# An mLSTM mixer on one core: loads in other shapes, a planner with later landings, priorities for each batch

## The chip, the cores and the metric

The kernel runs on one core of one Trainium2 chip. The time is device microseconds of the whole run. The core has five engines that each work off a list of instructions in order: TensorE (PE in the profile, with its weight loads as PEld), VectorE (DVE), ScalarE (ACT), GpSimd (POOL) and SyncE (SP), which here issues nearly all transfers. Transfers run on 16 DMA engines of the core. An instruction waits for semaphores of other engines or transfers, and all behind it on its engine wait with it.

## The reference

Four batches, eight heads, 768 tokens, 40 channels for each head. The first half is an mLSTM: a recurrence over tokens with a 40x40 state for each head and gates with a running maximum. The second half is a mixer over tokens of rank 32 and an MLP of 320 to 1280 to 320 channels with a residual.

```python
for t in range(S):
    m_new = np.maximum(f_gate[:, :, t] + m, i_gate[:, :, t])
    f_stab = np.exp(f_gate[:, :, t] + m - m_new); i_stab = np.exp(i_gate[:, :, t] - m_new); m = m_new
    C = f_stab[:, :, None, None] * C + i_stab[:, :, None, None] * np.einsum('bhd,bhe->bhde', vt, kt)
    n = f_stab[:, :, None] * n + i_stab[:, :, None] * kt
    nq = np.einsum('bhd,bhd->bh', n, qt)[:, :, None]
    y[:, :, t] = sigmoid(o_gate[:, :, t]) * np.einsum('bhde,bhe->bhd', C, qt) / np.maximum(np.abs(nq), 1.0)
x = y as (B, S, H * D)
u = x + ((x.transpose(0, 2, 1) @ U) @ V).transpose(0, 2, 1)
out = u + np.maximum(u @ w_ch1, 0.0) @ w_ch2
```

## The kernel before, in words

The tokens of a batch are cut into two halves of 384 and six chunks of 128. Heads go in groups of 3, 3 and 2, so a batch has six pieces (group and half), and 16 units (head and half). For a unit, VectorE builds the triangle of decays with a scan (L784, tile dm), TensorE the scores (q and k, L767), VectorE weighs the scores with the decays (L788, tile wt), and TensorE multiplies the result with v (tile tk). For a piece, k and weighted v give the state (tiles v and C), q is multiplied with its decays (L732, from tile fd) and with the state, the numerator is normed (L840) and gated into x (L845). When all six pieces of a batch are in x, the mixer over tokens follows (L872, tile pst; L917, tile ut), and then the MLP for each half of the batch: ten blocks of an up product (eight matmuls of ut with w1), a ReLU in a high part (ACT, L954) and a low part (DVE, L956), and three down products of three matmuls each (h with w2). Weights come as 64-bit words and are made into two 32-bit parts on ACT and DVE (L535 to L540, then L584, L585, L609).

Transfers: the token data of a piece (tk, L671, 544 or 363 KB), q of a piece (L676), q and k of a head and half (L756, 40 rows of 768 words, two of them side by side in tile qk), the decays of q of a piece (L729), the decays of a unit as one row copied to 128 partitions (L776), weights (L518). The gates are worked out first, for all batches, and stored: the decays of q in the DRAM tensor gsd (L463), those of the units in fsd (L444). The matrix V is stored once in DRAM (L559, tensor vsd) and read back in four copies (L569). The first 16 units take their decays from TensorE (L772) instead of a transfer.

The order of the instructions on all engines is made by a planner when the kernel is built (class Plan). Every operation has a kind, a priority, the engines it can run on, and a cost in ns. The planner steps through time, starts the ready operation of the lowest priority number on the engine that is free first, and writes each engine's list in the order of its own clock. An operation that both POOL and DVE can do goes to the one that would be done first. Where the planner expects TensorE to be idle or under-used, it puts in products of zeros (tile zeros, called fillers here). Tables add an offset to a kind's priority: ORDER for all batches, ORDER0 for the first.

Of the kernel before, what the change touches and what calls it, by code (L numbers as in the profile page):

```python
# [53 lines left out]
ORDER = {  # L54
    "gate": 20.0, "gate_w": 7.3, "part2": -70.0, "out_norm": -30.0, "part1": -10.0, "gate_turn": 10.0,
    "part3": -10.6, "rest1": 2.0, "w_low": 30.0, "vi": -10.0, "state": -4.0, "load_tk": -20.0, "load_qk": 0.9,
    "load_decay": -20.3, "w13_low": -30.0, "x_low": 24.0, "rows": -12.2, "inter": -1.6, "weigh": 1.8,
    "scores": 1.7, "weight_sign": -24.3, "weight_tail": 4.3, "cols": 21.8, "ut_high": 32.4, "store": 5.0,
    "decay_exp": -0.1,
}  # L60
ORDER0 = {
    "gate_w": 19.3, "part3": -44.0, "load_tk": 17.0, "load_q": -1.4, "x_low": -10.0, "rows": 25.0, "inter":
    -27.5, "weigh": 10.0, "scores": -4.1, "q_decay": 2.8, "weight_rebase": -20.9, "weight_sign": -23.3,
    "cols": 32.8, "store_g": 32.7, "residual": -7.0, "w_high": -27.4,
}
# [1035 lines left out]
```

## Time and profile before

| | us |
|---|---|
| runs of the kernel, median of 3 | 420.89 (420.51 to 435.31) |
| the profiled execution, whole | 416.58 |
| its span, first to last instruction | 414.8 |
| TensorE busy in the span | 393.2 |
| VectorE busy | 258.1 |
| GpSimd busy | 82.6 |
| mean granted TensorE clock | 0.97 of full speed |

A busy TensorE may be working at half its clock, or on fillers; both count as busy. A share of DMA is the mean over 16 engines: 0.20 is as much as three engines at work all the time and thirteen idle. The engines' queues run in order, so an engine's idle time has one cause at a time, the last thing that its next instruction waited for. Idle time of an engine off the longest chain costs nothing.

### The profile page before, as it was taken

What the parts mean: (1) busy time and instruction counts of PE and PEld (TensorE: products, weight loads), DVE (VectorE), ACT (ScalarE), POOL (GpSimd) and SP (SyncE); (2) the same over time, 40 slices, a digit from 0 to 9 for tenths busy, and PEclk for the clock granted to TensorE, in tenths of its full rate; (3) what the DMA queues carried; (4) which work ended last, traced back from release to release, by engine and by line L of the source; (5) the groups of instructions that cost most, each with busy time, mean ns of one, the idle gap of its engine ahead of it and who ended that gap; (6) DMA issues with size and microseconds to landing.
All of it is one profiled execution on the core that took longest, in us unless ns stands there. A gap on an engine that the chain in (4) does not pass through costs nothing.

```text
span 414.8 us, 7420 instructions
## 1 busy us (share of the span) xinstructions
PE 393.2 (95%) x2798; PEld 368.5 (89%) x2798; DVE 258.1 (62%) x534; ACT 124.6 (30%) x317; POOL 82.6 (20%) x96
## 2 busy tenths in 40 slices
PE   7995999998989999998899999999999999999995
PEld 5874888877888999987788999999999999999995
DVE  5996576999999965388798965328731233322132
ACT  4610323546345413212224232212421322111120
POOL 1652633125151600034323500003100000000000
PEclk9999558999999999999999999999999999999999
DMA  8746586867785361049665663102000010100001
GB/s 225 234 108 187 134 235 201 258 194 204 197 261 175 84 195 56 0 138 253 207 215 177 190 189 73 49 0 81 2 0 2 0 49 0 49 0 2 32 17 48
DMA packets 27260, 48.95 MB, mean 118 GB/s; under 512 B 3865, under 2 KB 18841, under 8 KB 27225
## 3 DMA queue, kind: packets, MB, share of 16 engines
q1 hardware_dynamic: 27032, 48.08, 40.4%
q8 instruction: 22, 0.36, 0.4%
q10 hardware_dynamic: 192, 0.40, 0.3%
q14 instruction: 14, 0.11, 0.1%
HBM read 44.24 MB, written 4.23 MB: 117 GB/s over the span
## 4 chain that ended last, share of the span: by engine, by line
PE 66%; DVE 16%; DMA 10%; issue 4%; ACT 1%; SPq 0%; POOL 0%; DVEq 0%; POOLq 0%; ACTq 0%
PE ps L301 66%; DMA tk<-in_tk 5%; DVE dm L784 4%; DMA q<-in_q 2%; DVE wt L788 2%; DMA qk<-in_qk 2%; DVE cv L538 1%; DMA raw<-in_w 1%; DVE cv L540 1%; DVE C L718 1%; DVE h L956 1%; DVE cv L536 1%; ACT C L704 0%; DVE x L450 0%; DVE q L732 0%
## 5 line engine op out<-in xcount | busy, mean ns | idle before, releaser
L301 PE MATMUL ps<-ut,w1h 128*128 128x384 f32 x400 | 120.9, 342 | 0.6 <-DVE h L956 0.4
L301 PE MATMUL ps<-w2h,h 128*128 128x320 f32 x480 | 120.3, 311 | 0.0
L956 DVE SCALAR_TENSOR_TENSOR h<-ps,h 128x384 fp32r<-128x384 f32 x80 | 43.7, 551 | 86.5 <-ACT h L954 86.2
L301 PEld LDWEIGHTS ps<-w2h,h 128*128 128x128 f32 x480 | 83.6, 188 | 0.5
L301 PE MATMUL ps<-ut,w1l 128*128 128x384 f32 x240 | 80.7, 336 | 0.0
L954 ACT ACTIVATE h<-ps 128x384 fp32r<-128x384 f32 x80 | 39.0, 490 | 135.0 <-PE ps L301 134.7
L301 PEld LDWEIGHTS ps<-ut,w1h 128*128 128x128 f32 x400 | 73.7, 188 | 1.8 <-DVE h L956 0.7
L301 PE MATMUL ps<-w2l,h 128*128 128x320 f32 x240 | 74.0, 308 | 0.1
L301 PE MATMUL ps<-tk,wt 128*128 128x82 f32 x384 | 55.0, 287 | 6.0 <-DVE wt L788 5.4
L301 PEld LDWEIGHTS ps<-tk,wt 128*128 128x128 f32 x384 | 51.2, 204 | 10.3 <-DVE wt L788 7.8
L784 DVE TENSOR_TENSOR_SCAN dm<-fd,ident 128x384 f32<-128x384 f32 x48 | 47.9, 1007 | 2.5 <-DMA fd<-fsd 2.4
L301 PEld LDWEIGHTS ps<-w2l,h 128*128 128x128 f32 x240 | 45.1, 188 | 0.4 <-DVE w2l L585 0.4
L301 PEld LDWEIGHTS ps<-ut,w1l 128*128 128x128 f32 x240 | 45.1, 188 | 0.0
L679 POOL TENSOR_TENSOR v<-tk,tok 128x369 f32<-128x369 f32 (+1 forms) x20 | 17.0, 850 | 117.8 <-PE ps L301 53.0
L301 PE MATMUL ps<-qk 40*128 40x128 f32 x384 | 33.9, 304 | 1.1 <-DVE dm L784 0.8
L788 DVE TENSOR_TENSOR wt<-ps,dm 128x384 f32<-128x384 f32 x64 | 33.3, 540 | 1.6 <-PE ps L301 1.6
L301 PEld LDWEIGHTS ps<-qk 40*128 40x128 f32 x384 | 27.2, 199 | 6.6 <-issue 1.9
L301 PE MATMUL ps<-zeros 128*128 128x256 bf16 x222 | 31.5, 287 | 1.6 <-DVE x L415 1.1
L301 PEld LDWEIGHTS <-zeros 128*128 128x128 bf16 x222 | 21.3, 103 | 7.3 <-issue 1.8
L979 DVE TENSOR_TENSOR o<-ps,x 128x320 f32<-128x320 f32 x24 | 11.2, 490 | 22.5 <-PE ps L301 22.5
L704 ACT ACTIVATE C<-ps,cst 120x123 f32<-120x123 f32 (+3 forms) x58 | 16.1, 343 | 27.5 <-PE ps L301 26.8
L301 PE MATMUL ps<-v,tk 128*120 128x123 f32 (+1 forms) x120 | 17.3, 278 | 4.5 <-POOL v L679 4.2
(95 smaller groups left out, 426.0 us busy)
## 6 DMA issues: line engine op xcount, KB each, us to landing
fd<-fsd SPq DMA_DIRECT2D x48, 192.0 KB
tk<-in_tk SPq DMA_DIRECT2D x16, 544.5 KB
qk<-in_qk SPq DMA_DIRECT2D x64, 120.0 KB
raw<-in_w SPq DMA_DIRECT2D x20, 320.0 KB
out<-o SPq DMA_DIRECT2D x24, 160.0 KB
tk<-in_tk SPq DMA_DIRECT2D x8, 363.0 KB
q<-in_q SPq DMA_DIRECT2D x16, 180.0 KB
fd<-gsd SPq DMA_DIRECT2D x12, 120.0 KB
```

The costliest lines, as they stand in the source:

```text
L301: nc.tensor.matmul(o, a, b, start=start, stop=stop, **kw)
L536: p.op("weight_shift", pri, "dve", 69 + n / 1.92, lambda tu=tu: V.tensor_scalar(tu(), tu(), 4, 1, ALU.logical_shift_left, ALU.logical_shif ...
L538: p.op("weight_sign", pri, "dve", dve(n), lambda tu=tu, hi=hi: V.scalar_tensor_tensor(tu(), hi(), 0x80000000, tu(), ALU.bitwise_and, ALU.b ...
L540: p.op("weight_tail", pri, "dve", dve(n), lambda tu=tu, lo=lo: V.scalar_tensor_tensor(tu(), lo(), 29, tu(), ALU.logical_shift_right, ALU.b ...
L679: p.op("v2", at(n - 1), ("pool", "dve"), (pool(3 * wd) * 0.83, dve(3 * wd)), lambda e: e.tensor_mul(v2v(), vtv(), tokv(1, gi, hf, DV)), r= ...
L704: nc.scalar.activation(grid(T[kc], 3, wd)[0:r, 0:nk, hs], ps[:, :, hs], AF.Copy, scale=col)
L718: nc.vector.scalar_tensor_tensor(cv(c), cv(c - 1), dec, cv(c), ALU.mult, ALU.add)
L784: lambda kfb=kfb, kdm=kdm: nc.vector.tensor_tensor_scan(T[kdm], T[kfb][:, 0:HS], ident3.rearrange("p c t -> p (c t)"), 0.0, ALU.mult, ALU. ...
L788: p.op("weigh", at(u), "dve", dve(HS), lambda ks=ks, kw=kw, kdm=kdm: nc.vector.tensor_mul(T[kw], T[ks][:, 0:HS], T[kdm]), r=[ks, kdm], w=[ ...
L954: p.op("relu_high", pri + m - 1000, "act", 371, lambda: nc.scalar.activation(T[kh][:, 0, :], T[kp][:, 0:HS], AF.Relu), r=[kp], w=[(kh, 0)] ...
L956: p.op("relu_low", pri + m - 1000, "dve", dve(HS), lambda: nc.vector.scalar_tensor_tensor(T[kh][:, 1, :], T[kp][:, 0:HS], 0.0, f32(T[kh][: ...
L979: p.op("residual", pri - 1000, "dve", dve(DM), lambda: nc.vector.tensor_add(T[ko], T[ka][:, 0:DM], T[X][:, tt, 0:DM]), r=[ka] + [(X, hf, g ...
```

## The change

- The decays of q are stored five times (tensor gsd has a new dimension of D // 8 = 5), and each stored row is read eight times in place of forty.
- V is stored four times, and read back without copying.
- q and k of a head are loaded as 48 rows in place of 40 (the rows behind are there in the input already, and no product reads them).
- The planner takes 1900 ns from the end of a transfer's data to its landing (950 before), 245 bytes per ns for the data (270 before), and charges the store of the decays and that of V by other sizes; the load of V is no longer taken as a wide one.
- The priorities get one offset for each kind and each of the four batches, from a table of 76 rows; ORDER0 goes. Ties between engines are now broken in a fixed order.

```diff
+DQ = 48
 ORDER = {
-    "gate": 20.0, "gate_w": 7.3, "part2": -70.0, "out_norm": -30.0, "part1": -10.0, "gate_turn": 10.0,
...
+    "load_tk": (-225.88, -307.52, 734.05, -157.5),
...
+def PRI(kind, batch):
+    return ORDER.get(kind, (0.0,) * 4)[batch]
-BEGIN, COLD = 600.0, 7000.0
+BEGIN, COLD, LAND = 600.0, 7000.0, 1900.0
-        pri += ORDER.get(kind, 0.0) + (ORDER0.get(kind, 0.0) if self.batch == 0 else 0.0)
+        pri += PRI(kind, self.batch)
-            for e, c in picks.items():
+            for e in [e for e in ("pe", "act", "dve", "pool", "sp", "aq") if e in picks]:
+                c = picks[e]
-                end[n] = dma + 950.0
+                end[n] = dma + LAND
-    vsd = dram.tile([RANK, S], F32, name="vsd")
+    vsd = dram.tile([P // RANK, RANK, S], F32, name="vsd")
-    gsd = dram.tile([NBH, S], F32, name="gsd")
+    gsd = dram.tile([NBH, D // 8, S], F32, name="gsd")
-        return nbytes / 270.0
+        return nbytes / 245.0
-                lambda hs=slice(hf * HS, (hf + 1) * HS), g=g: nc.sync.dma_start(out=gsd[:, hs], in_=g()),
+                lambda hs=slice(hf * HS, (hf + 1) * HS), g=g: nc.sync.dma_start(out=gsd[:, :, hs], in_=g().unsqueeze(1).to_broadcast([NBH, D // 8, HS])),
-            out=vsd.rearrange("r (a n) -> (r a) n", n=VN), in_=t()), r=[kc], w=[("vsd",)])
+            out=vsd.rearrange("c r (a n) -> (r a) c n", n=VN), in_=t().unsqueeze(1).to_broadcast([P, P // RANK, VN])), r=[kc], w=[("vsd",)])
-                nc.sync.dma_start(out=v4(), in_=vsd[:, cs].unsqueeze(0).to_broadcast([P // RANK, RANK, HS]))
+                nc.sync.dma_start(out=v4(), in_=vsd.rearrange("c r s -> (c r) s")[:, cs])
-                rows = gsd[b * NHEAD + h0:b * NHEAD + h0 + nh, hf * HS + c0 * P:(hf + 1) * HS]
-                nc.sync.dma_start(out=T[kgb][0:r, tg], in_=rows.unsqueeze(1).to_broadcast([nh, D, HS - c0 * P]))
+                rows = gsd[b * NHEAD + h0:b * NHEAD + h0 + nh, :, hf * HS + c0 * P:(hf + 1) * HS].rearrange("h a s -> (h a) s")
+                nc.sync.dma_start(out=T[kgb][0:r, tg], in_=rows.unsqueeze(1).to_broadcast([nh * D // 8, 8, HS - c0 * P]))
-                                out=T[kqk][64 * i:64 * i + D].rearrange("p n s -> p (n s)"), in_=qk[b, h + i, hf, 0:D],
+                                out=T[kqk][64 * i:64 * i + DQ].rearrange("p n s -> p (n s)"), in_=qk[b, h + i, hf, 0:DQ],
```

The lists of all engines come out in another order. Line numbers of the change are 77 above those of before. Three places show it.

SyncE, the first transfers of the program, before (x is the gates, qk the q and k of a head, tk the token data of a piece, q3 its q, fsd and gsd the two stores of decays):

```order
L382 DMA x_0_82<-in_fig 32x768
L671 DMA tk_0_95<-in_tk 128x1089
L676 DMA q3_0_100<-in_q3 120x384
L756 DMA qk_0_107<-in_qk 40x768 x2
L671 DMA tk_1_96<-in_tk 128x1089
L756 DMA qk_1_108<-in_qk 40x768 x2
L676 DMA q3_1_101<-in_q3 120x384
L756 DMA qk_2_109<-in_qk 40x768 x2
L444 DMA fsd_74<-x_1_83 32x384
L671 DMA tk_2_97<-in_tk 128x726
L463 DMA gsd_75<-x_2_84 32x384
```

And with the change:

```order
L459 DMA x_0_82<-in_fig 32x768
L833 DMA qk_0_107<-in_qk 48x768 x2
L833 DMA qk_1_108<-in_qk 48x768 x2
L833 DMA qk_2_109<-in_qk 48x768 x2
L748 DMA tk_0_95<-in_tk 128x1089
L748 DMA tk_1_96<-in_tk 128x1089
L748 DMA tk_2_97<-in_tk 128x726
L748 DMA tk_3_98<-in_tk 128x1089
L595 DMA raw_0_123<-in_u_w 128x6x64
L595 DMA raw_1_124<-in_v_w 128x384
L753 DMA q3_0_100<-in_q3 120x384
L753 DMA q3_1_101<-in_q3 120x384
```

All four buffers of tk are now filled before U, V (raw) and q3, and the first decays are stored behind them.

SyncE further on, around the store of V (vsd) and the loads of the decays of q (fd from gsd), before:

```order
L729 DMA fd_3_117<-gsd_75 120x1x384
L729 DMA fd_0_114<-gsd_75 120x1x384
L756 DMA qk_0_107<-in_qk 40x768 x2
L729 DMA fd_1_115<-gsd_75 80x1x384
L671 DMA tk_0_95<-in_tk 128x1089
L676 DMA q3_1_101<-in_q3 120x384
L756 DMA qk_1_108<-in_qk 40x768 x2
L729 DMA fd_2_116<-gsd_75 120x1x256
L671 DMA tk_1_96<-in_tk 128x726
L676 DMA q3_0_100<-in_q3 120x384
L559 DMA vsd_73<-cv_1_130 128x192
```

And with the change:

```order
L636 DMA vsd_73<-cv_1_130 128x4x192
L806 DMA fd_0_114<-gsd_75 120x1x256
L806 DMA fd_1_115<-gsd_75 120x1x256
L806 DMA fd_2_116<-gsd_75 80x1x256
L806 DMA fd_3_117<-gsd_75 120x1x384
L833 DMA qk_0_107<-in_qk 48x768 x2
L833 DMA qk_1_108<-in_qk 48x768 x2
L646 DMA raw_2_125<-vsd_73 128x384
L646 DMA raw_0_123<-vsd_73 128x384
L595 DMA raw_1_124<-in_w1 128x640
L806 DMA fd_0_114<-gsd_75 120x1x384
L753 DMA q3_0_100<-in_q3 80x384
```

V's store stood behind seven of the loads of decays of q, and now stands ahead of all of them; the load of tk for the batch's fifth piece (tk_0_95) stood fifth in the upper list, and is now the fourth row behind the end of the lower one.

GpSimd in the first batch (tk with rd is the norm L840, tk with tok the weighting of v L681, q3 with fd the decays of q), before:

```order
L840 TENSOR_TENSOR tk_0_95<-tk_0_95,rd_0_118 128x360
L679 TENSOR_TENSOR v2_0_99<-tk_3_98,tok1_70 128x369
L681 TENSOR_TENSOR tk_3_98<-tk_3_98,tok1_70 128x369
L732 TENSOR_TENSOR q3_0_100<-q3_0_100,fd_2_116 80x256
L840 TENSOR_TENSOR tk_1_96<-tk_1_96,rd_1_119 128x360
L554 TENSOR_TENSOR u4_80<-cv_0_129,u4_80 128x6x32
L679 TENSOR_TENSOR v2_0_99<-tk_0_95,tok1_70 128x369
L732 TENSOR_TENSOR q3_1_101<-q3_1_101,fd_3_117 120x384
L681 TENSOR_TENSOR tk_0_95<-tk_0_95,tok1_70 128x369
L840 TENSOR_TENSOR tk_2_97<-tk_2_97,rd_0_118 128x240
```

And with the change:

```order
L809 TENSOR_TENSOR q3_0_100<-q3_0_100,fd_0_114 120x256
L809 TENSOR_TENSOR q3_1_101<-q3_1_101,fd_1_115 120x256
L654 TENSOR_TENSOR vst_81<-raw_2_125,rru_0_94 128x384
L654 TENSOR_TENSOR vst_81<-raw_0_123,rru_0_94 128x384
L809 TENSOR_TENSOR q3_0_100<-q3_0_100,fd_2_116 80x256
L917 TENSOR_TENSOR tk_2_97<-tk_2_97,rd_0_118 128x240
L662 TENSOR_TENSOR w1l_77<-cv_2_131,w1h_76 128x320
L956 TENSOR_TENSOR h_0_87<-x_0_82,h_0_87 128x320
L756 TENSOR_TENSOR v2_0_99<-tk_1_96,tok1_70 128x246
L758 TENSOR_TENSOR tk_1_96<-tk_1_96,tok1_70 128x246
```

The norm and the weighting of v of most pieces have gone from GpSimd to VectorE's list; over the whole program GpSimd has 34 instructions fewer and VectorE as many more.

## Rows read from the trace of the kernel before

**Rows 1.** The page, parts 1 and 2: span, busy time of each engine, granted clock in 40 slices.

```profile
span 414.8 us, 7420 instructions
PE 393.2 (95%) x2798; PEld 368.5 (89%) x2798; DVE 258.1 (62%) x534; ACT 124.6 (30%) x317; POOL 82.6 (20%) x96
PEclk9999558999999999999999999999999999999999
```

**Rows 2.** Stretches: length; busy us of PE, PEld, DVE, ACT, POOL; clock; DMA share; GB/s.

```profile
0.00:5.00 5.00, 3.94 (x23) 2.98 (x24) 1.10 (x5) 2.95 (x5) 1.06 (x7) 1.00 0.67 171
5.00:35.00 30.00, 27.77 (x245) 22.61 (x244) 28.37 (x62) 11.35 (x35) 13.65 (x16) 1.00 0.70 196
35.00:45.00 10.00, 5.75 (x39) 4.80 (x39) 4.53 (x9) 0.85 (x3) 3.06 (x4) 0.83 0.52 160
45.00:70.00 25.00, 24.66 (x137) 20.96 (x137) 17.18 (x32) 7.89 (x24) 10.45 (x13) 0.59 0.76 200
70.00:141.90 71.90, 67.22 (x520) 60.59 (x519) 70.04 (x150) 35.53 (x91) 24.13 (x25) 1.00 0.69 199
180.00:245.00 65.00, 60.35 (x496) 55.42 (x495) 57.12 (x119) 19.84 (x60) 23.90 (x25) 1.00 0.72 210
245.00:414.80 169.80, 165.40 (x1085) 163.85 (x1084) 59.25 (x118) 36.00 (x79) 4.83 (x5) 1.00 0.09 26
```

**Rows 3.** The chain of waits, 29 to 41 us: start, length, what.

```profile
29.08 11.25 DMA tk<-in_tk
40.47 0.81 POOL v L679
```

**Rows 4.** Four shorter stretches, same columns as rows 2.

```profile
16.50:18.00 1.50, 1.50 (x15) 1.40 (x13) 1.50 (x3) 1.03 (x4) 1.42 (x2) 1.00 0.68 246
36.00:36.60 0.60, 0.60 (x7) 0.60 (x7) 0.60 (x1) 0.00 (x0) 0.00 (x0) 1.00 0.20 68
37.00:41.30 4.30, 0.10 (x1) 0.00 (x0) 1.10 (x2) 0.51 (x1) 0.83 (x2) 1.00 0.56 180
41.80:65.50 23.70, 23.70 (x117) 19.93 (x115) 15.07 (x28) 5.76 (x17) 9.84 (x13) 0.50 0.74 195
```

**Rows 5.** GpSimd, 21 to 24 us: start, length, instruction, idle before and releaser.

```profile
21.57 0.75 POOL L732 TENSOR_TENSOR q<-q,fd 120x256 f32<-120x256 f32 x1 [2.04 <-DMA gsd<-x]
23.45 1.08 POOL L732 TENSOR_TENSOR q<-q,fd 120x256 f32<-120x256 f32 x1 [0.16 <-DMA fd<-gsd]
```

**Rows 6.** Groups by form: count, busy us, mean ns of one, idle before.

```profile
L784 DVE TENSOR_TENSOR_SCAN dm<-fd,ident 128x384 f32<-128x384 f32 x48 | 47.9, 1007 | 2.5 <-DMA fd<-fsd 2.4
L540 DVE SCALAR_TENSOR_TENSOR cv<-raw,cv 128x320 uint32<-128x320 uint32 x20 | 11.9, 597 | 0.0
L681 DVE TENSOR_TENSOR tk<-tk,tok 128x369 f32<-128x369 f32 x6 | 3.3, 550 | 0.7 <-POOL v L679 0.7
L840 POOL TENSOR_TENSOR tk<-tk,rd 128x360 f32<-128x360 f32 x12 | 11.0, 916 | 25.9 <-DVE rd L836 23.7 <-ACT ut L915 2.3
```

**Rows 7.** Two lines of VectorE: count, ns min/median/max, first and last start.

```profile
L784 DVE TENSOR_TENSOR_SCAN dm<-fd,ident x48: 889/944/1676, 62.0 to 291.2; 128x384 f32<-128x384 f32 x48
L540 DVE SCALAR_TENSOR_TENSOR cv<-raw,cv x22: 348/478/1166, 30.4 to 135.9; 128x320 uint32<-128x320 uint32 x20, 128x192 uint32<-128x192 uint32 x2
```

**Rows 8.** The low parts of the hidden layer until 142.1 us, same columns.

```profile
L956 DVE SCALAR_TENSOR_TENSOR h<-ps,h x10: 521/539/558, 99.0 to 141.9; 128x384 fp32r<-128x384 f32 x10
```

**Rows 9.** TensorE, fillers and one block: start, length, instruction, count.

```profile
66.31 2.58 PE L301 MATMUL ps<-zeros 128*128 128x256 bf16 x22
...
360.87 0.34 PE L301 MATMUL ps<-ut,w1h 128*128 128x384 f32 x1
...
362.29 0.31 PE L301 MATMUL ps<-w2h,h 128*128 128x320 f32 x1
...
363.60 0.34 PE L301 MATMUL ps<-ut,w1h 128*128 128x384 f32 x1
```

**Rows 10.** The chain of waits near 193 us.

```profile
192.91 9.29 DMA tk<-in_tk
```

More of the change, by code (lines that the diff above doesn't have):

```diff
@@ L54 @@
 ORDER = {
-    "gate": 20.0, "gate_w": 7.3, "part2": -70.0, "out_norm": -30.0, "part1": -10.0, "gate_turn": 10.0,
[L56 to L59, printed above, removed]
-}
[L61 to L65, printed above, removed]
@@ L66 @@
-BEGIN, COLD = 600.0, 7000.0
+    "load_gates0": (-779.7, 0.0, 0.0, 0.0),
+    "load_consts": (597.19, 0.0, 0.0, 0.0),
+    "load_gates1": (35.83, 0.0, 0.0, 0.0),
+    "gate_consts": (371.85, 0.0, 0.0, 0.0),
+    "gate_start": (-223.71, 0.0, 0.0, 0.0),
+    "gate_max": (-74.85, 0.0, 0.0, 0.0),
+    "gate_shift": (-7.25, 0.0, 0.0, 0.0),
+    "gate_diff": (-766.66, 0.0, 0.0, 0.0),
+    "gate_exp": (265.83, 0.0, 0.0, 0.0),
+    "gate_input": (632.07, 0.0, 0.0, 0.0),
+    "gate_input_exp": (13.25, 0.0, 0.0, 0.0),
@@ new lines @@
+    "idents": (371.18, 0.0, 0.0, 0.0),
+    "gate_ends": (-190.6, 0.0, 0.0, 0.0),
+    "decay_high": (110.69, 0.0, 0.0, 0.0),
+    "decay_low": (1005.5, 0.0, 0.0, 0.0),
+    "store_decay": (-90.76, 0.0, 0.0, 0.0),
+    "gate_w": (-430.39, 0.0, 0.0, 0.0),
+    "gate_w_mul": (-391.91, 0.0, 0.0, 0.0),
+    "gate_g": (-164.87, 0.0, 0.0, 0.0),
+    "store_g": (885.38, 0.0, 0.0, 0.0),
+    "gate_turn": (672.42, 0.0, 0.0, 0.0),
+    "gate_keep": (917.48, 0.0, 0.0, 0.0),
+    "gate_total": (395.42, 0.0, 0.0, 0.0),
@@ new lines @@
+    "totals": (-97.19, 0.0, 0.0, 0.0),
+    "totals_keep": (206.22, 0.0, 0.0, 0.0),
+    "load_weights": (-136.48, 0.0, 0.0, 0.0),
+    "weight_rebase": (-472.39, 0.0, 0.0, 0.0),
+    "weight_shift": (-309.83, 0.0, 0.0, 0.0),
+    "weight_sign": (-839.8, 0.0, 0.0, 0.0),
+    "weight_tail": (53.0, 0.0, 0.0, 0.0),
+    "u_high": (581.35, 0.0, 0.0, 0.0),
+    "u_low": (-41.14, 0.0, 0.0, 0.0),
+    "store_v": (513.2, 0.0, 0.0, 0.0),
+    "load_v": (-85.69, 0.0, 0.0, 0.0),
+    "v_high": (363.73, 0.0, 0.0, 0.0),
@@ new lines @@
+    "v_low": (229.12, 0.0, 0.0, 0.0),
+    "w_high": (740.34, 0.0, 0.0, 0.0),
+    "w_low": (-35.91, 0.0, 0.0, 0.0),
+    "w13_high": (697.27, 0.0, 0.0, 0.0),
+    "w13_low": (-668.37, 0.0, 0.0, 0.0),
+    "load_tk": (-225.88, -307.52, 734.05, -157.5),
+    "load_q": (402.85, 50.85, 393.49, -511.12),
+    "v2": (350.11, 189.06, -478.77, 312.01),
+    "vi": (-311.57, 879.06, 413.73, -517.8),
+    "sigmoid": (-948.73, 1151.6, 458.69, 460.49),
+    "kv": (-466.34, -235.54, -14.01, -237.5),
+    "kv_mask": (664.68, 842.99, -233.56, 123.69),
@@ new lines @@
+    "state": (-76.96, -16.49, 179.79, 92.55),
+    "load_g": (-1094.17, -598.18, -169.93, -623.22),
+    "q_decay": (-647.59, -140.38, -312.64, 618.21),
+    "load_qk": (-682.42, 462.68, 418.05, -1035.57),
+    "scores": (167.22, -177.34, 171.89, 515.47),
+    "decay": (229.79, 0.0, 0.0, 0.0),
+    "decay_scan": (223.28, 231.52, 1377.54, 62.14),
+    "weigh": (-340.85, -99.95, 135.82, -363.81),
+    "pv": (462.8, -341.7, -890.0, -148.84),
+    "inter": (-392.52, 265.9, -1163.92, 226.89),
+    "norm": (-237.33, -339.01, -97.78, 418.51),
@@ new lines @@
+    "out_norm": (9.13, -119.33, -530.27, -232.09),
+    "gate": (-101.46, -120.32, 578.57, -19.58),
+    "again": (-634.42, 22.26, -97.97, -173.71),
+    "x_high": (-946.94, 742.48, 1043.87, -206.18),
+    "x_low": (404.1, 492.93, -406.35, 159.4),
+    "rows": (424.91, 45.76, -93.26, -456.1),
+    "rows_high": (860.09, -748.43, -517.83, -596.94),
+    "rows_low": (-859.1, 361.87, 617.68, -1036.12),
+    "rows_low2": (-1165.81, 726.06, 333.68, -995.35),
+    "cols": (-100.09, -395.82, 441.92, 264.29),
@@ new lines @@
+    "ut_high": (837.18, 59.41, -103.61, 182.22),
+    "ut_low": (-575.73, -355.95, -368.62, -41.3),
+    "ut2_high": (-1082.83, 581.02, 477.41, 330.5),
+    "ut2_low": (-242.24, 268.66, 751.75, 140.8),
+    "load_decay": (0.0, 297.66, 616.96, 844.87),
+    "up": (-8.38, -311.38, 268.56, 87.63),
+    "relu_high": (-308.15, 1009.89, 15.11, 51.11),
+    "relu_low": (-460.38, 497.18, -1160.75, 352.51),
+    "down": (-4.8, 246.93, 564.63, 685.69),
+    "residual": (445.06, -290.63, 412.82, -1142.22),
@@ L67 @@
+    "store": (64.92, -135.68, -1271.97, -145.26),
+}
+def PRI(kind, batch):
+    return ORDER.get(kind, (0.0,) * 4)[batch]
+BEGIN, COLD, LAND = 600.0, 7000.0, 1900.0
 DELTA = {"pe": 0}
@@ L442, in gates @@
             p.op(
-                "store_decay", pr + 30, "sp", dma(NBH * HS * 4),
+                "store_decay", pr + 30, "sp", dma(D // 8 * NBH * HS * 4),
                 lambda hs=slice(hf * HS, (hf + 1) * HS), fs=fs: nc.sync.dma_start(out=fsd[:, hs], in_=fs(0, HS)),
@@ L557, in keep_v @@
     def keep_v(pri, kc, t):
-        p.op("store_v", pri, "sp", dma(P * VN * 4), lambda: nc.sync.dma_start(
-            out=vsd.rearrange("r (a n) -> (r a) n", n=VN), in_=t()), r=[kc], w=[("vsd",)])
+        p.op("store_v", pri, "sp", dma(P // RANK * P * VN * 4), lambda: nc.sync.dma_start(
+            out=vsd.rearrange("c r (a n) -> (r a) c n", n=VN), in_=t().unsqueeze(1).to_broadcast([P, P // RANK, VN])), r=[kc], w=[("vsd",)])
         for c in range(2):
@@ L568, in load @@
             def load(cs=cs, v4=v4):
-                nc.sync.dma_start(out=v4(), in_=vsd[:, cs].unsqueeze(0).to_broadcast([P // RANK, RANK, HS]))
-            p.op("load_v", pri, "sp", dma(P * HS * 4), load, r=[("vsd",)], w=[k4], new=[(k4, "raw")], load=0)
+                nc.sync.dma_start(out=v4(), in_=vsd.rearrange("c r s -> (c r) s")[:, cs])
+            p.op("load_v", pri, "sp", dma(P * HS * 4), load, r=[("vsd",)], w=[k4], new=[(k4, "raw")])
             p.op(
@@ L756, in load_qk @@
                             nc.sync.dma_start(
-                                out=T[kqk][64 * i:64 * i + D].rearrange("p n s -> p (n s)"), in_=qk[b, h + i, hf, 0:D],
+                                out=T[kqk][64 * i:64 * i + DQ].rearrange("p n s -> p (n s)"), in_=qk[b, h + i, hf, 0:DQ],
                             )
-                        p.op("load_qk", at(u) - 7, "sp", dma(D * 2 * HS * 4), load_qk, w=[(kqk, i)], new=[(kqk, "qk")] if i == 0 else [])
+                        p.op("load_qk", at(u) - 7, "sp", dma(DQ * 2 * HS * 4), load_qk, w=[(kqk, i)], new=[(kqk, "qk")] if i == 0 else [])
                     def scmm(pair=pair, kqk=kqk):
```

## The prediction

> **What bounds the kernel now.** I read the page first, then a table of stretches, then the chain of waits where the table shows a hole, and at last single lines for prices. The page [rows 1] says TensorE is busy 393.2 of 414.8 us, so nothing but TensorE seems to matter; but its clock row has a dent, slices 5 to 7 at about half speed, and its busy time holds fillers. The stretches [rows 2] tell more. From 245 us on TensorE has no gap but the last store: 165.4 busy of 169.8. From 5 to 35 and from 70 to 141.9 us VectorE is the full engine: 28.37 of 30.00 and 70.04 of 71.90. Between them, 35 to 70 us, neither is: VectorE works 4.53 of 10.00 and 17.18 of 25.00.
>
> That hole has one beginning. The chain [rows 3] shows a transfer of tk issued at 29.08 that is not there before 40.4; GpSimd then weights v, and TensorE goes on at 41.3. Its idle 4.2 us (the third row of [rows 4]) are followed by 23.7 us at a granted clock of 0.50, which is 1.2 GHz in place of 2.4 (the last row there). VectorE starves in that time too, since it waits for scores.
>
> Why that transfer took 11.25 us: at 36 us, while tk was waited for, the DMA share was 0.20, three engines of sixteen (the second row of [rows 4]). Two loads of decays of q, each 120 rows of 1 KB, came in 1.88 us apart, 21.57 and 23.45 [rows 5]; that is 65 GB/s, where the stretch of 5 to 35 us moved 196 [rows 2]. These loads are of three heads by forty copies and run on three engines; behind them on the same three stands a share of every other transfer. The short stretch in which the 40-row loads of q and k run has a share of 0.68, eleven engines (the first row of [rows 4]).
>
> The Trainium skill has the rule: "DMA: Bandwidth & Descriptors", section "Why a DMA increments its semaphore by 16 and not by 1", says a transfer is spread over the largest count up to 16 that divides the slowest dimension of both sides. By it the old loads of decays get 3 and 2 engines and the 40-row loads 10, which the shares of 0.20 and 0.68 bear out, and the new ones 15, 10 and 16. No row here shows a transfer of the new shapes.
>
> **The change part by part.** I take a landmark that both programs pass: the tenth low part of the hidden layer on VectorE, which starts at 141.9 us [rows 8]. Up to there VectorE sets the time, behind it TensorE does.
>
> *VectorE's work up to the landmark.* Counted in the order of each program, it is 254 instructions before and 257 now. Twenty are new there, nearly all taken from GpSimd, or weights made earlier: at 0.55 [rows 6] (L681) or a little less, 10.5 us. Missing are four scans at about 1 us [rows 6], two weighings, four steps of weights and some small ones, done later now, 9.5 us, and one product of the mixer's weights (vst) that goes the other way, to GpSimd, 0.5. Difference: 10.5 - 9.5 - 0.5 = +0.5 us.
>
> *VectorE's waits up to the landmark.* In rows 2 its idle time is 3.90, 1.63, 5.47, 7.82 and 1.86, in sum 20.7. If the loads of decays spread over more engines than three, and four tk loads stand at the top of SyncE's list, the wait of 35 to 45 us goes, and with it the half clock: 5.5 + 7.8 = -13.3. What is late next in that stretch is VectorE itself; in its full stretches it still idles 1.63 of 30 and 1.86 of 72, 2.6 to 5.4%. On 22 us that is 1.2 at most: +1.2. The bound on the other side is that the whole 13.3 comes back (rival below).
>
> *GpSimd and VectorE.* The mean scan takes 1007 ns and its median 944; the mean weight step L540 takes 597, its median 478 [rows 6, 7]. Over 48 and 20 instructions that is 3.0 and 2.4 us; with the two other weight steps and the state updates I estimate some 11 us in all that are lost beside GpSimd's 82.6 us [rows 1]. Up to the landmark GpSimd now has 19 instructions less, at 0.92 [rows 6] (L840) 17.5 us. In proportion VectorE gets 11 x 17.5/82.6 = 2.3 back. Bounds 0 and 4; I take -2.0.
>
> The Trainium skill makes more of it: "SBUF — State Buffer", section "Who interferes with whom", calls the shared port pair an exclusive lock that blocks the loser for the whole instruction. By that each of the 19 could free VectorE for its full 0.92, and the sum would be 15 us lower than mine; the medians above say that most meetings cost nothing.
>
> *TensorE behind the landmark.* At its 80th up matmul the new order has more left: 12 records of scores, 12 of state products, 9 transposes, 4 products with U, 3 with pst, 18 down matmuls, and 16 fillers. A block of eight up matmuls takes 360.87 to 362.29, nine down matmuls 1.31 [rows 9]; the 18 are 2.6. The other 40 I price at the mean spacing of the mixed stretch 70 to 141.9, 67.22/520 = 0.129 [rows 2]: 5.2. Fillers take 2.58/22 = 0.117 [rows 9]: 1.9. Sum +9.7. In all there are 276 fillers where there were 222; the other 38 lie ahead of the landmark, 4.5 us, where TensorE has room as long as its clock is whole.
>
> *TensorE's waits behind it.* From 180 to 245 us it idles 4.65 [rows 2]; one cause is a tk transfer of 9.29 us [rows 10]. The new order spreads the attention of batches 2 and 3 over more of the MLP. Bounds: all of it goes, or none; I take half, -2.3.
>
> *Transfers.* 64 loads grow by a fifth, 1.5 MB, and the stores by 0.7 MB: 2.2 MB at 200 GB/s [rows 2] are 11 us of transfer, over 240 us whose share is about 0.7. Hidden as long as no engine of the sixteen is full. V's loads lie beside other work and cost nothing on the path.
>
> Sum: 0.5 - 13.3 + 1.2 - 2.0 + 9.7 - 2.3 = -6.2. Against the profiled execution: span 414.8 to 408.6, its own time 416.6 to 410.4. The median of the runs stands 4.3 above that execution; I take the same 6.2 off it: 414.7 us.
>
> **The rivals.**
>
> *More comes off.* The late waits are of the same kind as the early one (tk behind loads on three engines), and GpSimd's meetings cost the upper bound. Then -13.3 + 0.5 - 4 + 9.7 - 4.7 = -11.8: 409.1. For: rows 10 beside rows 3. Against: the 9.7 us of work left over are counted, not guessed. Chance 0.26.
>
> *The hole moves.* SyncE's list has V's store ahead of all loads of decays, and it stands until VectorE has made V's two parts, some 40 instructions into its list. Everything behind it is late, the fifth tk as well: 14 entries, about 3 MB, at 200 GB/s 15 us. If that store goes out later than about 28 us, tk lands behind 43, where VectorE should want it; TensorE then idles some 4 us and falls to half clock as it did at 41.8. The 13.3 are not won, the 9.7 are paid: 0.5 - 2.0 + 9.7 = +8.2, 429.1, and with nothing back from GpSimd 431. Against: VectorE's rows ahead of it add up to 22 us or so after its start at 4. Chance 0.12, half of it beyond 2%.
>
> *The shapes do nothing,* and transfers still crowd on three engines; only the earlier tk loads help. Half of the 13.3 stays: 421. Against: in [rows 4] the number of engines at work goes with the shape of the load, three for three heads by forty copies and eleven for forty rows, and the loads now have more rows of their own. Chance 0.12.
>
> **How the numbers follow.** My own case has 0.50 and runs from 409 to 419 (the waits between 0 and 5, the bounds of GpSimd and of the late half). Two per cent, about what a measurement of this kernel can tell from no change, is 8.4 us: faster is below 412.5, slower above 429.3. A quarter of my case and the first rival lie below: 0.39. Half of the third case is above: 0.06, and 0.02 for what I don't see: 0.08. Within: 0.53. For 8 in 10 the range takes in the first rival but for its end and the shapes that do nothing, and leaves out the moved hole: 405.5 to 424.
>
> **What would show it.** Right: a clock row without a dent; no wait for tk over 3 us before 140; the tenth low part at 126 to 131 us; VectorE idle some 8 us ahead of it; GpSimd at about 52 us, VectorE at 270 or less; TensorE's busy time near 387 with more fillers. Wrong: a half clock anywhere, a fifth tk that lands behind 43, a share near 0.2 while decays of q load, or VectorE short of full before the landmark with transfers at a share of 1.

## The result

The changed kernel takes 398.04 us (median of 4, 397.76 to 398.36), against 420.7 of before in the same comparison (median of 4, 415.98 to 435.31). The ratio is 0.950, 95% interval 0.942 to 0.958; here and below a ratio leaves out executions that are over 1.5% above the fastest of their kernel, while medians and ranges are of all. The forecast of 414.7 was 16.7 us too high, and 398 lies below its range. The direction was right, the size was not: 22.7 us came off where 6.2 were forecast.

The page of the changed kernel, its first parts, answers to [rows 1]:

```profile
span 396.2 us, 7570 instructions
PE 383.7 (97%) x2852; PEld 362.6 (92%) x2852; DVE 264.7 (67%) x570; ACT 124.5 (31%) x314; POOL 50.4 (13%) x62
PEclk9999999999999999999999999999999999999999
```

The dent in the clock row (PEclk, the granted clock of TensorE in 40 slices) is gone. GpSimd works 50.4 us where 82.6 stood and VectorE 264.7 where 258.1 stood, both near what was forecast. The stretches, same columns as [rows 2]; the last two are cut at the end of the span:

```profile
5.00:35.00 30.00, 28.71 (x258) 23.52 (x255) 29.30 (x59) 12.03 (x36) 6.97 (x9) 1.00 0.81 236
35.00:45.00 10.00, 10.00 (x88) 8.17 (x87) 9.80 (x21) 2.48 (x10) 3.56 (x5) 1.00 1.04 254
45.00:70.00 25.00, 24.66 (x220) 21.96 (x219) 24.19 (x58) 14.38 (x41) 8.71 (x9) 1.00 0.96 247
180.00:245.00 65.00, 64.81 (x476) 62.99 (x476) 38.49 (x84) 16.43 (x42) 4.70 (x5) 1.00 0.40 118
245.00:396.20 151.20, 147.81 (x1033) 144.80 (x1032) 70.69 (x148) 35.22 (x83) 6.21 (x8) 1.00 0.18 54
```

From 35 to 70 us, where VectorE had worked 21.7 of 35 us, it now works 34.0, at a whole clock, while the transfers run at a share of 1.04 and 0.96. From 180 to 245 us TensorE's 4.65 us of idle time are down to 0.19, and VectorE's load there fell from 57.12 to 38.49.

In the chain of waits from 20 to 70 us (start, length, what) no transfer is left where [rows 3] had one of 11.25 us:

```profile
26.69 3.89 PE ps L378 x33
30.59 14.31 PE ps L378 x127
...
48.04 14.14 PE ps L378 x129
```

The fifth load of tk, for which the forecast feared, is issued at 35.95 and is not waited for by TensorE. The landmark, the tenth low part on VectorE, starts at 123.28 us instead of 141.9 [rows 8] (VectorE's timeline):

```profile
123.28 0.54 DVE L1033 SCALAR_TENSOR_TENSOR h<-ps,h 128x384 fp32r<-128x384 f32 x1
```

So the program splits into two pieces. Before, then changed, each up to the landmark and behind it (the stretches again):

```profile
0.00:141.90 141.90, 129.33 (x958) 111.94 (x958) 121.22 (x253) 58.57 (x154) 52.35 (x65) 0.92 0.69 195
141.90:414.80 272.90, 263.85 (x1843) 256.56 (x1841) 136.83 (x282) 66.02 (x163) 30.26 (x32) 1.00 0.27 78
```

```profile
0.00:123.28 123.28, 115.17 (x945) 100.34 (x946) 116.81 (x257) 55.11 (x147) 32.39 (x42) 1.00 0.81 225
123.28:396.20 272.92, 268.55 (x1909) 262.25 (x1907) 147.91 (x315) 69.43 (x168) 18.00 (x20) 1.00 0.29 86
```

The whole 18.6 us came off ahead of the landmark; behind it the time is the same to 0.02 us, 272.90 and 272.92. That is not because nothing changed there: TensorE is busy 4.7 us longer (66 records more) and idle 4.7 us less, and it is chance that the two cancel.

### The profile page after: what moved, and what is told of

Its sections match the earlier page's. It is cut to its first block, busy times and chain, and to the rows that moved or that the text cites. A ratio compares the mean times of both kernels' runs of the same rounds, so it can differ in the third digit from the quotient of the medians.

```text
span 396.2 us, 7570 instructions
## 1 busy us (share of the span) xinstructions
PE 383.7 (97%) x2852; PEld 362.6 (92%) x2852; DVE 264.7 (67%) x570; ACT 124.5 (31%) x314; POOL 50.4 (13%) x62
## 4 chain that ended last, share of the span: by engine, by line
PE 81%; DVE 13%; issue 2%; DMA 2%; ACT 1%; SPq 0%; DVEq 0%
PE ps L378 81%; DVE dm L861 2%; DVE cv L615 1%; DVE C L795 1%; DVE wt L865 1%; DVE tk L758 1%; DVE cv L617 1%; DMA x<-in_fig 1%; DVE x L527 1%; DMA qk<-in_qk 1%; DVE tk L917 1%; DVE q L809 1%; DVE x L497 1%; DVE h L1033 0%; DVE cv L613 0%
## 5 line engine op out<-in xcount | busy, mean ns | idle before, releaser
L378 PE MATMUL ps<-tk,wt 128*128 128x82 f32 x384 | 50.8, 272 | 0.7 <-DVE wt L865 0.5
L378 PEld LDWEIGHTS ps<-tk,wt 128*128 128x128 f32 x384 | 47.8, 191 | 3.3 <-DVE wt L865 1.4
L861 DVE TENSOR_TENSOR_SCAN dm<-fd,ident 128x384 f32<-128x384 f32 x48 | 44.9, 949 | 0.0
L378 PE MATMUL ps<-zeros 128*128 128x256 bf16 x276 | 38.5, 280 | 5.4 <-DVE wt L865 2.2
L378 PEld LDWEIGHTS <-zeros 128*128 128x128 bf16 x276 | 26.1, 101 | 12.2 <-issue 6.6
L756 POOL TENSOR_TENSOR v<-tk,tok 128x369 f32<-128x369 f32 (+1 forms) x16 | 13.9, 867 | 136.9 <-PE ps L378 122.5
L378 PE MATMUL ps<-qk 40*128 40x128 f32 x384 | 29.8, 288 | 0.1
L378 PEld LDWEIGHTS ps<-qk 40*128 40x128 f32 x384 | 24.1, 187 | 4.9 <-issue 3.0
L781 ACT ACTIVATE C<-ps,cst 120x82 f32<-120x82 f32 (+3 forms) x55 | 15.3, 346 | 31.3 <-PE ps L378 31.1
L378 PE MATMUL ps<-C,q 120*128 120x123 f32 (+1 forms) x120 | 17.8, 279 | 0.0
```

The costliest lines, as they stand in the source:

```text
L378: nc.tensor.matmul(o, a, b, start=start, stop=stop, **kw)
L756: p.op("v2", at(n - 1), ("pool", "dve"), (pool(3 * wd) * 0.83, dve(3 * wd)), lambda e: e.tensor_mul(v2v(), vtv(), tokv(1, gi, hf, DV)), r= ...
L781: nc.scalar.activation(grid(T[kc], 3, wd)[0:r, 0:nk, hs], ps[:, :, hs], AF.Copy, scale=col)
L861: lambda kfb=kfb, kdm=kdm: nc.vector.tensor_tensor_scan(T[kdm], T[kfb][:, 0:HS], ident3.rearrange("p c t -> p (c t)"), 0.0, ALU.mult, ALU. ...
```

## The experiments

Where a kernel is built on the kernel before or on the changed one, all engines' lists stay as they are in it unless told otherwise. "Before" in a comparison is the kernel before in the same runs; its medians there were 418.7, 415.7, 416.9 and 418.2 us.

**Shapes and order apart.** Four kernels. The first is the kernel before with the new shapes alone, and the second the changed kernel with the old ones. The third and fourth are the kernel before with one of the three shapes. Lines are shortened here, and the store of each tensor changes with its shape:

```diff
 e1, on the kernel before (e2 is the reverse, on the changed kernel)
-gsd = dram.tile([NBH, S], F32, name="gsd")
+gsd = dram.tile([NBH, D // 8, S], F32, name="gsd")
...
-in_=rows.unsqueeze(1).to_broadcast([nh, D, HS - c0 * P])
+in_=rows.unsqueeze(1).to_broadcast([nh * D // 8, 8, HS - c0 * P])
-vsd = dram.tile([RANK, S], F32, name="vsd")
+vsd = dram.tile([P // RANK, RANK, S], F32, name="vsd")
...
-in_=qk[b, h + i, hf, 0:D]
+in_=qk[b, h + i, hf, 0:DQ]
```

> The kernel before, all engines' lists as they were; only the transfers have the new shapes (decays of q stored five times, V four times, q and k in 48 rows). Theory A (the shapes carry the gain: the tk transfer issued at 29.08 us is no longer caught behind three engines): the wait of 4.3 us before 41.3 and the half clock from 41.8 to 65.5 go, 13.3 us come off and some of the late idle too: 403 to 409 us against some 420. Theory B (the new order carries it: four tk loads ahead of everything, GpSimd's work moved to VectorE): the same transfer is still waited for, since it is still issued at 29; 414 to 421 us, with the dent in the clock. Theory C (each needs the other): 412 to 421.

> The changed kernel, all engines' lists as they are, with the old shapes of the transfers (decays of q stored once, V once, q and k in 40 rows). Theory A: tk, q3 and qk transfers are again caught behind the loads of decays on three engines; at least one wait of some us in the first 70 us, followed by a half clock: 410 to 420 us. Theory B: the early tk loads have landed before any load of decays is issued, no wait, clock whole: 398 to 403. Theory C: 408 to 421.

> The kernel before with only the decays of q stored five times and read in the new shape, order unchanged. Theory A in its narrow form (it is these loads alone that catch tk on three engines): nearly all of what the shapes give, within 3 us of the kernel with all shapes. If instead the 40-row loads of q and k (ten engines) hold tk up, this gives 0 to 4 us off the kernel before.

> The kernel before with only q and k loaded in 48 rows, order unchanged. Theory A narrow: the wait for tk stays, 0 to 3 us off the kernel before. If the loads of q and k are what matters (64 loads on ten of sixteen engines, the six others idle): 5 to 13 us off.

| kernel | median (range), us | ratio to before | span of the profile, us |
|---|---|---|---|
| shapes only | 403.01 (400.99 to 406.45) | 0.970 (0.960 to 0.980) | 400.6 |
| order only | 407.42 (405.86 to 409.05) | 0.981 (0.971 to 0.991) | 404.0 |
| loads of decays only | 406.43 (401.92 to 420.36) | 0.970 (0.957 to 0.983) | 400.1 |
| 48 rows only | 424.70 (418.44 to 431.24) | 1.013 (0.996 to 1.030) | 416.6 |

By the spans the shapes take 14.2 us off, the order 10.8, and both together 18.6, not 25.0: they remove the same hole in two ways. Theory A holds for the shapes, at the lower end of its 403 to 409; two other executions of shapes only have mean granted clocks of 0.974 and 0.983, so its clock still falls somewhere in some of them. For the order alone 407.42 lies between the ranges of theory A (410 to 420) and B (398 to 403): the wait and the dent that A expected are there, but the kernel is faster. Theory C, that each needs the other, fell. In the narrow form it is the loads of decays alone: their row has the ratio of the first, 0.970. The loads in 48 rows give nothing measurable. V's shape was not run by itself; the first and third row leave no gain for it that these runs could tell from noise.

The load of tk itself shows the cause. GpSimd's weighting of v waits for it. With the loads of decays alone in the new shape it is issued at 28.1 us, and GpSimd starts at 33.40; with the 48 rows alone it is issued at 29.7, and GpSimd starts at 41.27, as late as in the kernel before (GpSimd's timelines, in this order):

```profile
33.40 0.81 POOL L679 TENSOR_TENSOR v<-tk,tok 128x369 f32<-128x369 f32 x1 [1.53 <-DMA tk<-in_tk]
41.27 0.81 POOL L679 TENSOR_TENSOR v<-tk,tok 128x369 f32<-128x369 f32 x1 [10.09 <-DMA tk<-in_tk]
```

The pieces of shapes only, split at its landmark, and its stretch from 180 us:

```profile
0.00:127.98 127.98, 120.01 (x958) 103.99 (x959) 118.02 (x254) 59.21 (x154) 53.96 (x65) 1.00 0.84 229
127.98:400.60 272.62, 263.86 (x1843) 256.68 (x1841) 137.39 (x282) 65.96 (x163) 29.05 (x32) 1.00 0.28 81
180.00:245.00 65.00, 60.28 (x458) 56.55 (x457) 51.60 (x106) 19.82 (x55) 16.34 (x18) 1.00 0.69 185
```

And those of order only:

```profile
0.00:131.38 131.38, 117.70 (x945) 101.90 (x946) 116.64 (x257) 55.32 (x147) 31.91 (x42) 0.97 0.68 199
131.38:404.00 272.62, 268.41 (x1909) 262.04 (x1907) 147.83 (x315) 69.50 (x168) 18.37 (x20) 1.00 0.27 84
180.00:245.00 65.00, 64.81 (x475) 62.98 (x474) 42.88 (x95) 17.07 (x44) 5.50 (x6) 1.00 0.46 142
```

The last row of each tells whether the shapes made the late waits. With new shapes and the old order TensorE idles 4.72 us from 180 to 245, as before (4.65); with old shapes and the new order 0.19. So the old shapes did not make those waits, and the order removed them. TensorE's waits in the shapes-only kernel (from 125 us; line, waited for, sum in us, times, longest) name the engine that it waited for:

```profile
PE ps L301 <- DVE wt L788: 3.9, 4, 1.9
```

VectorE works 51.60 to 57.12 us of 65 there in the old order, and 38 to 43 in the new one, which puts the rest behind 245 us. It was not full in the old order either: among its own waits from 180 to 245 are these for transfers, two rows of the kernel before and two of shapes only:

```profile
DVE q L732 <- DMA q<-in_q: 2.5, 2, 1.6
DVE dm L784 <- DMA fd<-fsd: 2.4, 3, 1.4
DVE dm L784 <- DMA fd<-fsd: 2.5, 4, 1.1
DVE q L732 <- DMA q<-in_q: 1.2, 1, 1.2
```

So transfers have a part in the late waits, through VectorE. In order only VectorE waits 4.4 us for q in that stretch, and TensorE does not wait for it. How much of the gain there comes from VectorE's smaller load and how much from the other order of the work was not separated.

In order only the hole returns with another transfer. TensorE stands 6.2 us until 47.81, after q:

```profile
36.22 10.60 DMA q<-in_q
```

```profile
38.00:41.00 3.00, 3.00 (x33) 2.44 (x32) 3.00 (x6) 0.61 (x1) 0.47 (x1) 1.00 0.25 81
```

The first row is of the chain of waits, the second a stretch: the share is 0.25, four engines of sixteen, for these 3 of the 10.6 us that q is on its way (from 41 to 46 it is 0.93). In the changed kernel, where four loads of decays go out from 24.55 to 28.1, the share beside them is higher:

```profile
26.00:27.50 1.50, 1.46 (x18) 1.20 (x15) 1.50 (x4) 0.00 (x0) 0.00 (x0) 1.00 0.57 179
27.50:29.00 1.50, 1.50 (x13) 1.07 (x11) 1.50 (x4) 0.00 (x0) 0.74 (x1) 1.00 0.44 124
```

**One shape taken back in the changed kernel.** Each kernel undoes the two lines of its shape as above.

> The changed kernel with the decays of q stored once and read by forty copies of each head, the two other shapes new. If these loads are what delays the transfer of q in the changed order with all old shapes: a wait of some us near 37 to 47 us again, 404 to 409. If the 40-row loads do it: within 1 us of 398.

> The changed kernel with q and k in 40 rows, the other shapes new. DMA's share is full from 35 to 70 us in the changed kernel; if ten engines are too few there, VectorE waits for scores or TensorE for q: 400 to 405. If the transfers have slack: within 1 us of 398.

With the old loads of decays the changed kernel takes 406.23 us (405.73 to 407.56), with q and k in 40 rows 397.72 (397.24 to 398.47). Of the three shapes the loads of decays carry the gain in the new order too, 8.2 us; 40 rows are as good as 48, even where the share of DMA is full.

**Fillers, GpSimd and the planner.** Four edits of the changed kernel, lines shortened. With e8 the lists of all engines come out in another order; the other three leave the order of the program as it is.

```diff
 e5: the last 16 fillers left out
-mm(bank[:, 0:256], zeros[:, 0:P], zeros)
+p.held["fill"] += 1
+p.held["fill"] > 260 or mm(bank[:, 0:256], zeros[:, 0:P], zeros)
 e6: all norms on GpSimd (e7: v2 and vi on VectorE, in the same line)
-fn() if engs == eng else fn(ENGINE[eng])
+fn() if engs == eng else fn(ENGINE["pool" if self.kinds[n] == "out_norm" else eng])
 e8: the planner's constants of before
-BEGIN, COLD, LAND = 600.0, 7000.0, 1900.0
+BEGIN, COLD, LAND = 600.0, 7000.0, 950.0
-return nbytes / 245.0
+return nbytes / 270.0
```

> The changed kernel without its last 16 fillers (260 of 276 stay), all else in place. They stand behind the landmark, where TensorE is full. If a filler there costs what it takes (0.117 us each, as the prediction priced it): 396.1 us against 398.0. If they only fill waits: 398.0. If the clock needs them: a half clock of some us behind the place, 400 to 410.

> The changed kernel with all 21 norms that VectorE does (L917) given back to GpSimd at the same place in the program, 8 of them ahead of the landmark. VectorE is spared 8 x 0.50 = 4.0 us there, GpSimd works 8 x 0.86 = 6.9 us more. Theory P (VectorE loses a fraction of GpSimd's time, 7.5 of 32.4 us here): 4.0 - 1.6 = 2.4 us earlier, 395.6. Theory L (VectorE is blocked for the whole of each GpSimd instruction): 2.9 us later, 401, with VectorE's busy time ahead of the landmark no lower than 116.8. Theory W (the gating behind each norm waits for the slower engine): 2 to 5 us later, 400 to 403, with VectorE's busy time lower and its idle time before L922 higher by some us.

> The changed kernel with the 27 weightings of v that GpSimd does (L756, L758) given to VectorE at the same place, some 14 of them ahead of the landmark. Theory P: VectorE gets 14 x 0.5 = 7 us more and is spared 11 x 0.23 = 2.5: 4.5 us later, 402.5. Theory L: 7 more and 11 less, 4 us earlier, 394. Theory W: the weighted v is there earlier, which counts only where TensorE waits for it: between the two.

> The changed kernel with its shapes and its table of priorities, but the planner with the landing of 950 ns and 270 bytes per ns of before; the lists come out in another order on all engines. If the later landing is what puts the loads early enough: waits for transfers in the first 70 us, 402 to 415. If the table alone decides: 396 to 401. If table and landing fit only each other (a table made for one planner is any table for another): anything from 400 to 420, with waits that are not for transfers.

Without the late fillers: 397.04 us (396.78 to 397.2). Sixteen of them cost 1.0 us, not 1.9; the price of the prediction was about twice too high. Behind the landmark TensorE's busy time falls by 1.6 us (from 268.55) and its idle time rises by 0.4 (from 4.37), so some of the fillers only filled waits:

```profile
123.40:395.10 271.70, 266.94 (x1893) 260.80 (x1891) 147.59 (x315) 69.74 (x168) 19.52 (x20) 1.00 0.29 87
```

With the norms on GpSimd: 397.02 (396.84 to 397.46); the theories had 395.6 (P), 401 (L) and 400 to 403 (W), and none was met. The landmark is where it was, at 123.31:

```profile
0.00:123.31 123.31, 116.31 (x945) 102.16 (x946) 115.72 (x249) 55.14 (x147) 37.97 (x50) 0.99 0.82 224
```

VectorE gave up norms that are reckoned at 4.0 us and works only 1.1 less (116.81 to 115.72): by that its other instructions took 2.9 us longer beside 5.6 us more of GpSimd, about half, where theory P said a quarter and theory L all. Its idle time before L922 also rose to 1.6 us (theory W). What was won, 1.1 us, was won behind the landmark.

With v on VectorE: 400.71 us (400.48 to 414.23), 2.7 slower; theory P said 4.5 slower, theory L 4 faster. L is out as a sum, and P is too simple. The profile fell on the execution of 414.23. There TensorE waited 0.74 us for VectorE at 27.4, and its clock halved for some 30 us (the clock row, and PE's timeline):

```profile
PEclk9995569999999999999999999999999999999999
```

```profile
27.38 0.90 PE L378 MATMUL ps<-tk,wt 128*128 128x82 f32 x6 [0.74 <-DVE wt L865]
```

The other three executions of that kernel have a mean granted clock of 0.998 to 1.0. Why this one fell isn't shown; that so short a wait can stand in front of it is.

With the planner's old constants: 405.3 us (403.62 to 405.82). The waits of TensorE in it are for VectorE (wt 2.7 us) and ScalarE (w2h 1.9), none for a transfer, as the third theory said. With the older constants this table loses 7 us; a table made for them was not run.

The two edits that helped, in one kernel:

> The changed kernel with both edits that were a little faster: norms on GpSimd and without the last 16 fillers. Each took 1.0 us off behind the landmark; if they add up, 396.0 us, if they are the same time twice, 397.0.

396.43 us (395.94 to 397.87), the lowest median of all: 1.6 us of the 2.0 hoped for. The range takes in both expected values, 396.0 and 397.0, so whether the two gains add up is open.

**The half clock behind the hole.** Fillers are put ahead of the product that waits. This is the edit for the wait for q in the changed kernel with the old loads of decays (e13); in the kernel before (e9 and e14) 44 fillers stand ahead of the state product that waits for v:

```diff
+def bridge(n):
+    free = [sl for sl in p.slots["ps"] if sl[2] is None]
+    for _ in range(n):
+        mm(min(free, key=lambda sl: sl[1])[0][:, 0:256], zeros[:, 0:P], zeros)
...
-ps = grid(T[kn], 3, wd)
+ps = grid(T[kn], 3, wd); bridge(50 if (b, gi, hf) == (0, 2, 0) else 0)
```

> The kernel before with 44 more fillers ahead of the product that waits for v at 41.3 us; 44 at 0.11 us are 4.8 us, a little more than the wait of 4.2. The late transfer stays. Theory H (TensorE's idle time in the hole is what lowers the clock): no half clock from 41.8 to 65.5, the hole's own 4 to 5 us stay, some 7 us off, 409 against 416, and runs that scatter less. Rival (the clock falls in that place for something else, or the wait only comes back a little later): half clock as before, 416 to 417.

> The changed kernel with the old loads of decays (406.2 us: a wait of 3.9 us at 41.9 for q, then a clock of 0.5 until some 56 us), with 50 more fillers (5.5 us) ahead of the product that waits. Theory H (TensorE's idle time lowers the clock): the clock stays whole there, the wait itself stays, 2 to 5 us off: 401 to 404. Rival (the clock falls for something else, or the fillers cost what the clock gives): 405.5 to 408.

> The kernel before with 44 fillers ahead of the product that waits at 41.3 us, for one more profile. Theory H: in an execution whose clock is whole until 37 us it stays whole from 41.8 to 65.5, VectorE works more than 17.18 of the 25 us from 45 to 70, and the run takes 409 to 412 us. Rival: the dent is there as before, 415 to 417.

The kernel before with the bridge took 419.46 us (410.94 to 428.22, 10 runs), ratio 0.998 (0.990 to 1.005): no gain where 7 us were expected, and no less scatter. Its profile can't tell why, since there the clock had fallen at 11 us already. A second profiled execution, 410.19 us, can: the stretch of the bridge, and the one behind it,

```profile
42.00:47.00 5.00, 5.00 (x49) 4.52 (x48) 2.03 (x4) 0.40 (x1) 1.24 (x2) 1.00 0.25 82
47.00:70.00 23.00, 23.00 (x211) 19.61 (x209) 20.64 (x43) 11.95 (x34) 10.68 (x13) 1.00 0.87 246
```

have a whole clock where before had 0.50. So does the bridged wait for q. The changed kernel with the old loads of decays, and then the same with the bridge, from 45.8 to 56 us:

```profile
45.80:56.00 10.20, 9.33 (x37) 6.42 (x38) 4.97 (x12) 2.64 (x8) 2.52 (x3) 0.50 0.73 179
```

```profile
45.80:56.00 10.20, 8.97 (x73) 7.20 (x70) 6.20 (x14) 3.60 (x12) 4.30 (x6) 1.00 0.76 187
```

Theory H holds for the clock in both places: without the idle time it does not fall (one execution of the kernel before, and all four of the kernel with the wait for q, with mean granted clocks of 0.996 to 1.0 where 0.981 to 0.983 stood without the bridge). It fails for the price. The bridged kernel takes 405.29 us against 406.23, 0.9 less and not 2 to 5: near 50 us TensorE waits in either for VectorE's work on the next q, without the bridge and with it,

```profile
50.67 1.64 PE L378 MATMUL ps<-C,q 120*128 120x123 f32 x6 [0.86 <-DVE q L809]
50.12 0.93 PE L378 MATMUL ps<-C,q 120*128 120x123 f32 x6 [0.78 <-DVE q L814]
```

and the chain of the unbridged kernel leads to that q, 10.45 us from issue to landing; so the transfer set the time and the clock mattered little. The 410.19 us of the kernel before lie within the 409 to 412 of theory H, but the ten runs of that kernel show no gain. Its clock falls in other places too: in the execution of 410.19 us a wait of 1.24 us for q and k stands at 25.39, and the clock is half from 27 to 38.

```profile
25.39 1.01 PE L301 MATMUL ps<-qk 40*128 40x128 f32 x12 [1.24 <-DMA qk<-in_qk]
27.00:38.00 11.00, 11.00 (x56) 9.79 (x54) 6.21 (x15) 0.98 (x4) 4.02 (x6) 0.54 0.68 177
```

## Why the prediction was wrong

The mechanism of the hole was right: loads of decays on few engines hold up a transfer, TensorE stands, its clock halves, VectorE starves. The sizes were wrong, all on one side, in three places. The direction came out right for the reason given.

| step | forecast, us | measured, us |
|---|---|---|
| VectorE's work up to the landmark, GpSimd's share in it | +0.5 - 2.0 | -4.4 (121.22 to 116.81) |
| VectorE's waits up to there | -13.3 + 1.2 | -14.2 (20.68 to 6.47) |
| TensorE's work behind it | +9.7 | +4.7 |
| TensorE's waits behind it | -2.3 | -4.7 (9.05 to 4.37) |
| median above the profiled execution | +4.3 | 0.0 (398.03 and 398.04) |
| **together, against the 416.58 of the profiled execution** | -6.2 + 4.3 = -1.9 | -18.5 |

*Behind the landmark, 7.4 us of the miss.* The step that failed is "TensorE behind the landmark", +9.7 for 74 instructions, 40 of them at 0.129. The trace has 66 records more there, and they add 4.7 us, 0.07 each. The 0.129 is TensorE's busy time over its instructions in a stretch that also holds large products of the MLP, and it was too much for the small ones: twelve more scores add nothing. The fillers, too, cost 1.0 us for 16 where 1.9 stood. And a product that both programs have equally often there, an up product with w1h, takes 2.7 us less with the change; why, isn't shown. Groups by form behind the landmark, before and changed (count, busy us, mean ns of one, idle before):

```profile
L301 PE MATMUL ps<-qk 40*128 40x128 f32 x192 | 15.3, 289 | 0.0
L378 PE MATMUL ps<-qk 40*128 40x128 f32 x204 | 15.3, 286 | 0.0
L301 PE MATMUL ps<-ut,w1h 128*128 128x384 f32 x350 | 105.7, 341 | 0.0
L378 PE MATMUL ps<-ut,w1h 128*128 128x384 f32 x350 | 103.0, 340 | 0.8 <-DVE ut L1000 0.8
```

The other part is the choice of "half" of the late waits: -2.3 where -4.7 was measured. I put them down to tk transfers on the strength of one row [rows 10] and halved them for doubt. TensorE waited there for VectorE, which in its turn waited for q, decays and tk now and then; the new shapes left these waits, and the new order removed nearly all of them from 180 to 245 us.

*Ahead of it, 5.0 us.* VectorE's waits were nearly right. Its work fell 3.2 us with the shapes alone, where every instruction and its engine is the same. That this is a smaller loss beside GpSimd isn't shown: GpSimd works no less ahead of the landmark there (52.35 and 53.96 us), and some groups of VectorE got shorter (a state step of 12, 5.6 to 4.6 us) while others got longer (a weights' step of 20, 11.6 to 12.6), so the cause of these 3.2 us stays open. The order took 1.2 more, near the forecast of 1.5. My bound of 4 us for the meetings came from GpSimd's amount of work; whether the measured fall, 4.9 beside the 0.5 of added work, lies beyond it is open with that.

*The anchor, 4.3 us.* I carried over the distance of the median from the profiled execution. It went with the clock: runs of the kernel before go from 411 to 435 us with mean granted clocks of 0.98 down to 0.93 where they were listed, and the changed kernel stays within 0.6 us at 0.994 to 1.0. Not all of that scatter comes from the hole: shapes only still goes from 401 to 406 us, and in one execution of the bridged kernel before the clock fell at 11 us.

*The rivals.* "More comes off" sized the late waits (-4.7) right for a wrong reason: the new shapes, which end the early wait, leave the late ones. Its 409.1 is still 11 us too high. "The hole moves" did not come: V's store goes out at 24.11. "The shapes do nothing" is refuted by shapes only. The rule that the slowest dimension of both sides sets how many engines a transfer uses ("DMA: Bandwidth & Descriptors", "Why a DMA increments its semaphore by 16 and not by 1", of the Trainium skill) agrees with the shares above as far as few engines against more go, 0.25 and 0.44 to 0.57. The counts of 15 and 10 engines that I worked out from it for the new loads can't be read from these shares, since other transfers run beside them. The lock rule ("SBUF — State Buffer", "Who interferes with whom", of the Trainium skill) has the loser blocked for the whole instruction. Theory L went further and took VectorE for the loser of every meeting; the kernel with the norms on GpSimd shows a loss of about half of GpSimd's added time, and the one with v on VectorE was slower where theory L has it faster. Which engine lost each single meeting isn't shown.

Two readings of mine proved less than I took from them. The share of 0.20 [rows 4] held for 0.6 us; from 30 to 35 us, with tk on its way, it was 0.90. What shows the cause is the kernel with the loads of decays alone. And I took the 1.88 us between GpSimd's two products [rows 5] for the rate of the old loads; in the changed kernel they are 1.89 apart (27.53 and 29.42), though the loads have the new shape.

## What to carry to other kernels

Price added work by its own kind, from rows of the same product where its engine is full, never by a mean over a stretch that mixes small products and large ones. For every late wait look at which engine released it, and then at what that engine had waited for, before blaming a transfer; one row of the chain of waits does not settle it. If the times of a kernel scatter, look for stalls and falls of the clock: when a change removes some, the sum has to be made against one execution whose stalls are in view, and no distance of the median be added.
